# Block-sparse attention with a gated convolution feed-forward: mask rows copied in pieces, first loads in another turn, closing blocks in halves, and a new written order

## The chip, the core and the metric

The kernel is written for one core of a Trainium2 chip. A core has five engines that run side by side, each through its own list of instructions and strictly in that list's order: TensorE (PE: matrix products, with PEld for the loading of their weights), VectorE (DVE), ScalarE (ACT), GpSimd (POOL) and SyncE (SP). Here SP and POOL mainly start transfers between the memory and the core. Between engines only semaphores hold an instruction back. The metric is device time in microseconds (us) from the first to the last instruction of one launch, and what lies around it; the median over runs is compared.

## The reference

Attention over 4 batches, 8 heads, 768 positions and 64 numbers a head, with a mask of 32 by 32 blocks. Its output, heads side by side (512 numbers a position), goes through a feed-forward with a convolution over three neighbouring positions in its gate:

```python
scores = scale * np.matmul(q, k.transpose(0, 1, 3, 2))
...
mask = np.abs(blk_i - blk_j) <= window
mask = mask | (blk_i == 0) | (blk_j == 0) | (blk_i == n_blocks - 1) | (blk_j == n_blocks - 1)
for qb in range(n_blocks):
    for kb in sampled_blocks[qb]:
        mask[qb * block:(qb + 1) * block, kb * block:(kb + 1) * block] = True
...
attn = attn / (np.sum(attn, axis=-1, keepdims=True) + 1e-09)
return np.matmul(attn, v)
...
h = np.maximum(x @ w_in, 0.0)
...
for k in range(K):
    conv_out += conv_w[k][None, None, :] * hp[:, k:k + S, :]
gate = 1.0 / (1.0 + np.exp(-conv_out))
return (h * gate @ w_out)
```

The inputs and the output are in float32. The three sampled blocks of each row of blocks are drawn at random and are read by the kernel.

## The kernel before

Two heads make a pair; there are 16 pairs, four to a batch. For each pair a slot tensor `T_t` (five of them, 88 partitions by 24 by 128 in bf16) holds the transposed q in its first 12 chunks and the transposed k in its last 12, each in partitions 0 to 63. Partitions 64 to 87 hold 24 mask rows: one-hot block numbers of the keys, and for the queries a large negative number wherever a block is masked, so that one product over 88 rows gives masked scores. The mask rows depend on no head. They are built once in slot 0 and then copied to the other slots: `m_slot` (line 350) is one DVE copy of all 24 chunks for each of slots 1 to 4.

The queries of a batch are taken in two halves of 384 positions (g = 0 and 1; a chunk of q with an even number belongs to g = 0). In the first four pairs q and k come through POOL's transfers (`ld_k`, `ld_q`, `ld_v`, and `ld_q` again for g = 1), are transposed by PE (`k_tr`, `q_tr`) into a PSUM bank (`mix`, two of them) and copied from there into the slot (`k_cp`, `q_cp`, on DVE or ACT). The first pair is special: its q and k come in float32 through SP's and ACT's own transfers, are cast (`cast_q`, `cast_k`) and transposed head by head. Pairs 4 and 5 go the same way as 1 to 3; later pairs are transposed by a transfer and copied by `stg_cp`.

The work is cut into 144 units. A unit is some four `s` products into a bank `st` of two (`L754`), one exponential `exp` of 128x1024 on ACT from there (`L766`), and eight products `av` with the values (`L791`) into a bank `av` of two. The first 18 units are batch 0, g = 0, and 4.5 units belong to a pair: pair 1 begins in unit 4, pair 2 with unit 9 and pair 3 in unit 13. When the `av` of a pair are done, `rcp` and `norm` (`L700`, `L702`, DVE) divide by the sum and free the `av` bank; for the first segment `x_tr` and `x_cp` transpose the result on PE. After the four pairs of a segment come the feed-forward's first products `f1` (`L888`, bank `mix`), `relu` (DVE or ACT), the gate (`mul`, `add`, `tanh`, `g1`, `g2`), and the second products `f2` (`L823`), whose result `ev` copies to `o2s_t` and `out` sends to memory, 128 positions at a time.

Of the last batch the last block of 128 positions (t = 5) is made in two halves of 256 columns; blocks t = 3 and 4 are made whole. In the profile a group of `f2` in a whole block is 128x512, in a half 128x256.

No scheduler runs at build time. The order of all operations on all engines is written out in the string `ORDER`, two characters for an operation, then the engine where there is a choice (P, A, V, G) and the numbers of the buffers it takes. `put_down` (line 93) emits them in this order; within an engine the instructions stand as they do in the string. The lists of POOL and SP are part of it. At the start PE runs 42 products on zeros (`warm`, `fill`).

Of the kernel before, what the change touches and what calls it, by code (L numbers as in the profile page):

```python
# [25 lines left out]
6h1Z15U06u36z46C16D6i16q6r6E56L06v6M6w6A6B6j26k1+V1j5VV1n1/V6F6Q16R6G6l06N06S16O06V06P6W6H06I6mV6J16KV6X26T6+16U6/
ih070373074iiik1754181pijV00il7c1imV7d7e52b07h0in17iio6Y7j01s4V2U24W1t7m17n7o12cViF02dViGipV1iIiH4X2W24Y2X4Z1u4+1v
4/31050iq0ir7r06Z717s72767A1isA7t2iJiN17B7C32w12xV4781iO2yV771iz0iA7F07GiBA27H47f7g7k2p07K12z17L7l7p7q7P07Q7u7v2qV
2rViP79iK7M5it0iu7D07U12AV7w22BV2HV4ivV3iQ7V7R03337W17E7I7J7a17bV1iR810822K0832861iS2LV02MV7x877Niw17O7S7T883ixiL
iyV8b08c7X7Z07Y1847y0858g18d48hiM0iT7zV7+2N1898a8p08qiC08eiV22OV2PV2VV0iWiU8i58r08u18viD8f8z08A8w1102Y12Z02+3615134  # L30
373528B28j8k8s07/18E18F8t8x8y8J0iEV80V8l1j138miYj2iX8G38Kj908C8L48R18S8D8T58H8W08X8Ija8n18Y0j4iZ8/1908oV2/Vi+30Vj3
i/8M8N18U8V8Z94095jf1j5j08O291111962jg8+929c1939d9h09i97jbjh98j69e43c3d1523a1532C03f3e543l9m19nj732V1j83bV29901iji
jjV038V9j39o539V8P9ajc9r0jdA19sjo19w1jpjl09t0jqA9xjm9y1jnV3o9E09F9G23p03m22Q13rju19f09gjv9J19K2D09k9l9O09PjwA9L4jJ0
jLjK2EVjM9Q3jr19p9q2FVjNjO9T1jsjtVjR1jA09U9/0jB9ujS9V5jCA9vjx1jyjzAa09z9A1a41a59H9I9M2R09NjPjUjT9B1jZ29Cj/a10a619R
a90aa9S8Q29W9X2SVjV2TVjG1a20ae1jQj+ab2afjHa3jD0aj0a7aka8jWag4jEar1asal39Y2jIVk0jFVjXk539Zk1k6jYk8k7ackj1aw0axadahai
at0ay1amaB1aCan1aukv0avazaG0aHaD4k2aI3k9kak3k43q3h0jk9DaO1kk9baP3t13iaAkbao1kcaEaFkwaJaT0aKaL0aMaUkl3x3y03A3B2aQ5kx
aY1aV29+3u3s4ap3g3aq03jV3kVkykzA2kmaZb103D3C3Jb2knA3kB0kCkE1kFkDV14kGVkZ0k+a+0b313vVb61b7b84kN0kObe0aR1bfkQ1kRaSaW
aXk/kPA5bj1bkkK0bg3kSAbl5l0l1l2kLbo0kW1a/bpb0b4b5bt1b9buba0bq03M3N33K1aNbhld1kMVbv2kXbB0bCbikH0kYAbD13wVlf3nA3bG1kI
bb2lelg3zV4bckT1bmbnbr3P3OkJV6bH3UbI43F03Q13Gl52l7kUkVV7l3bL0bMl6bN3kp0kqbsbwbxbQ1bRbS5bV0bWbdkokrkd1bE1bX03R3E0ll3
lml8lol9lhlal41by1kAlblcbzlnlilpljc11ksbFbJbKbOc2c60c7c82ktA0bPbTbAkulk3HV3IVkekfkgc31cb0bUbYlt0lubZ0cccg1khA3lqlr  # L40
3LV0b+0lscd4lvlz1chlAco0cplBlCci3lwct1cuc4cq0lDA2lxA0cy0czc5lF13V03X3Y1403Zb/3+lGcv53SV13WV13TVlHVlI0lJcD1c9cElKV
m10m2m3cacem4m5cA1cF2lO1cfcI0cJcK4kilPlL0lMcjcklNAlQVm92ma410mbmcm6m7cl2cr1cQ1cRcS3cscwcV0cWcxcBcCcGcHlR0494a0c01ly
4f1c+1c/cX53/46472cLcN1mdd00lSd30d4lU1lVdb1dccOcmcncP42jelTAmelWVmh1mimjmfmkmgm84ed51dd2cM1cTcUcYcZlX0d1lYmllZVdg0
dhdi4l+1l/dl1d2dmd6d7dq0drm0Amp3de0d80dfdn34b4c4nds5mD1djdkdodpdv1dwdD0dEmx0mEmymmdx0mqd9msdtmrdudydz1dF2dI1dJmtmu
mnmo4o24s4ddGdHdN0dOdK4mvmzmFdadP34kdS1dTdLmwmGdMd+0d/dQmA4pdA24l143V2mHV344VmBV0dU5e31dRe4e00dVdWdX1dBe52e80e9mV1
mWea1mXV08dYmY0mZe10e2m+Vnh2ninknjed1ee4glEn21e6m/0ei0ejn0n34B4C34qef4ek3n4A4Geq1ere7ebecegehelev04r4y4Des0n1V9np0
nqnsnrewnl48V2en04hV3n51em1n6eteA1euex2n7Aa4t045dC2dZeBeon80mJ1eF0mKeGeC14z0n9mLnmeH4mMepeN1eOeS0eTmNA1naV4iV4mV34E
4F4MeP5ne0nb1nfeX1eyezeYeDeEeInx1nyntnzeU3nuf00eJncf1eZ04N24H1ngVnneK2eQ0eRmP0eVeWe+f514j4ueLeMf6f22ndAbe/f3fd0fe
f71mQmRnvno0nAnwnBnF3nGnInHfi1fjff4nCmC4vV4nD4wVnJf4mSmTA2nT1nUfn0fofk5f8f91fgo60o7fhfs1ftfp3fA0fBnK4Io8VnEmIfu0nL
fa1nMo30o4fC2flnVfmnWo5Vot2ouovowoxfb4AV4nXA0fF1fGfK0fLnN0nZ1nOfH1fM4oyfqfrnPn+n/AnQfP1fQo01fvo1nRA34JV04KVfwfU0fV  # L50
oz4OV0oAfR5oc0g01g1o2AfW3fx0fyol0omfD0fEfIfJodonoog20opoeAg50g6g72o91oaga1fNfOfSgbfTfXfY1gf0ggobVoB1oDoC4Loqgc1fZ2
oi0ojof1ognS4xnYgh4orosoEf+g3g4gn1g8gogs0ohAokAoFoJ3oKg9gp5gtmUfc0fzoR1gu3oX0gdoLgegigx1gyoMoNoGgjoSoHgG0gq0grgvgw
gHoYgz0gAgBgL1gMoOgI2gk1oIglgC0gN1oToZgQ0gRgS4f/gmoPoQo+gJ1o/A3mOgZ1oUg+h20h3g/5h43p70p8p9paoVV0pbV2h71h8gKpg1phpd0
p0pehg0gDgOpfV1cpiAhhh90pj1pm0pnhi2poAgPpkplAdhl1hmgThq0pp0gE1pqgUpB2pDpCpcpEpJ0pFhn1gFA1h00h1h5h6haps1pthbprAepGpK
pLpuAhrpMpv0hz1hApwhs4p11pHgV2gWhc1pNpxAfhB5hE0hdpR1pSpTpUp2gX0gYApOhj1hkp3p4hFpI1pVp5A1hG3hohphthuhN1py0he1pzhv0pP
hwhOhC0pQhfApAAhx1hDhHhW0hI1hyVqk0qlhP0hXpZ3hJ2p+p/pWqmAgqq1hQh/1qrhRq50hY2i0i80i9q6q0q1pXhKq2qsAhpYhS1q3q4hL1q7hZ0
q8i11ia4hMV2qh1qihTq9A3qB2qR0qCqDh+i2i31ibqn0qjAii40i5qt1qui61icid2qoi7Aqb1qcqpAjqwqviehU0qdhVVif0qeigAri0rjqJ3qEqx
qLqSqFqfA2r91raqyrkArbAqzqUrf0rgqGrc1rl0rmrhArA1rBp6qgoWqaqAqHqIrn1qKrorC2rdr30rv0rwrDrpreArq1rrrEqTqMrx1rs2qZ1rtqN
qOruryqVrzqPqQq+r4rR0rSrL1rMrNrOrTrUqWqXqYrPV1r5r6rVAr7A2q/r0rWrQr8r1V0r2rF0rGrHrIrJA3rK
# [52 lines left out]
def kernel(  # L112
# [207 lines left out]
    def dcopy(e, dst, src):  # L320
        if e == "ACT":
            nc.scalar.copy(out=dst, in_=src)  # L322
        elif e == "POOL":
            nc.gpsimd.tensor_copy(out=dst, in_=src)
        else:
            nc.vector.tensor_copy(out=dst, in_=src)  # L326
# [723 lines left out]
```

## Time and profile before

| what | value |
|---|---|
| time, median of 3 runs | 208.17 us (208.16 to 208.91) |
| the profiled execution's own time | 208.6 us |
| its span, first to last instruction | 206.6 us |
| mean granted clock of TensorE | 0.998 |
| busy: PE, DVE, ACT, POOL | 197.9, 187.0, 189.9, 61.1 us |
| instructions | 6225 |

The profile is a record of one execution. Its page gives busy times by engine, the span in 40 slices with the busy share in tenths, the transfers, and the chain of work that ended last. Further views show instructions in order of time (start, length, engine, line, operation, tiles; equal neighbours merged, in brackets the idle time before and what ended it), groups of instructions of one line and shape, and busy times in chosen stretches. Starts count from the first instruction.

### The profile page before, as it was taken

How to read it: one execution, taken by the hardware profiler on the slowest of the kernel's cores; microseconds unless marked ns; L12 is line 12 of the kernel's file. 1: busy time of each engine (PE TensorE's matmuls, PEld its weight loads, DVE VectorE, ACT ScalarE, POOL GpSimd, SP SyncE). 2: the span in 40 equal slices, each digit the busy share in tenths (PEclk: the TensorE clock that was granted, in tenths of full speed). 3: DMA queues.
4: the chain of work that ended last, by engine and by line, in shares of the span. 5: the costliest groups of instructions: out<-in, count | busy, mean ns of one | idle time of the engine just before them, and what ended most of it. 6: DMA issues, size and time to landing. Idle time of an engine off the chain costs nothing.

```text
span 206.6 us, 6225 instructions
## 1 busy us (share of the span) xinstructions
PE 197.9 (96%) x2400; PEld 142.8 (69%) x2418; DVE 187.0 (91%) x578; ACT 189.9 (92%) x250; POOL 61.1 (30%) x114
## 2 busy tenths in 40 slices
PE   7799999999999999999999999999999999999991
PEld 5577877787667766766576767676677767786750
DVE  7999999999999998999789989999999938999970
ACT  6999999999999999999979998999999979997841
POOL 8976655204353223217044153800000000000000
PEclk9999999999999999999999999999999999999999
DMA  6999999972949795999977659999133131010414
GB/s 160 179 196 188 187 172 132 156 127 41 113 59 184 109 194 87 145 151 173 194 98 98 142 76 181 138 137 162 47 111 91 22 121 51 3 51 5 152 54 152
DMA packets 49305, 25.00 MB, mean 121 GB/s; under 512 B 35100, under 2 KB 46332, under 8 KB 49276
## 3 DMA queue, kind: packets, MB, share of 16 engines
q0 software_dynamic: 20000, 11.24, 43.5%
q1 hardware_dynamic: 28988, 13.07, 30.2%
q8 instruction: 19, 0.31, 0.6%
q10 hardware_dynamic: 288, 0.30, 0.4%
q14 instruction: 10, 0.08, 0.2%
HBM read 23.09 MB, written 6.29 MB: 142 GB/s over the span
## 4 chain that ended last, share of the span: by engine, by line
PE 86%; DVE 5%; ACT 5%; issue 1%; another core or an unknown queue 1%; ACTq 0%
PE st L754 30%; PE mix L888 19%; PE mix L823 17%; PE av L791 17%; ACT pt L766 2%; DVE m L946 1%; DVE t L326 1%; PE mix L721 1%; ACT t L322 1%; PE st L823 1%; PE mix L517 1%; PE av L965 1%; ACT o2s L322 1%; DVE m L954 0%
## 5 line engine op out<-in xcount | busy, mean ns | idle before, releaser
L766 ACT ACTIVATE pt<-st 128x1024 bf16<-128x1024 f32 x144 | 140.3, 1036 | 2.6 <-PE st L754 1.8
L754 PE MATMUL st<-t 88*128 88x256 bf16 (+2 forms) x600 | 90.9, 268 | 1.8 <-ACT pt L766 0.7
L754 PEld LDWEIGHTS <-t 88*128 88x128 bf16 x600 | 48.2, 97 | 20.3 <-issue 2.2
L791 PEld LDWEIGHTS <-pt 128*128 128x128 bf16 x1152 | 52.8, 97 | 12.4 <-ACT pt L766 0.4
L791 PE MATMUL av<-vt,pt 128*128 128x65 bf16 x1152 | 58.9, 193 | 0.2
L888 PE MATMUL mix<-xT,winb 128*128 128x384 bf16 (+2 forms) x288 | 54.8, 308 | 0.3 <-ACT hE L908 0.2
L946 DVE TENSOR_SCALAR m<-hE,cw 128x382 bf16<-128x382 bf16 (+2 forms) x192 | 49.5, 317 | 0.4
L823 PE MATMUL mix<-woutb,gT 128*128 128x512 bf16 x166 | 45.3, 379 | 0.4
L954 DVE TENSOR_TENSOR m<-m 128x764 bf16<-128x764 bf16 (+2 forms) x64 | 33.8, 534 | 0.5
L888 PEld LDWEIGHTS <-winb 128*128 128x128 bf16 x288 | 24.1, 97 | 9.2 <-issue 0.8
L993 ACT ACTIVATE m<-m 128x764 bf16<-128x764 bf16 (+2 forms) x32 | 26.4, 830 | 1.3 <-DVE m L954 1.2
L823 PEld LDWEIGHTS <-gT 128*128 128x128 bf16 x200 | 17.4, 97 | 11.5 <-DVE gT L1001 0.6
L402 POOL COPY pace<-pt 1x1 bf16<-1x1 bf16 x24 | 8.4, 352 | 56.3 <-ACT pt L766 56.3
L910 DVE TENSOR_SCALAR hE<-mix 128x384 bf16<-128x384 f32 x29 | 16.0, 554 | 4.1 <-PE mix L888 3.2
L908 ACT ACTIVATE hE<-mix 128x384 bf16<-128x384 f32 (+2 forms) x35 | 17.1, 504 | 1.7 <-PE mix L888 1.7
L1001 DVE TENSOR_TENSOR gT<-m,hE 128x764 bf16<-128x764 bf16 (+3 forms) x36 | 18.2, 510 | 0.5
L702 DVE TENSOR_TENSOR xtok<-av,rcp 128x384 bf16<-128x384 f32 (+2 forms) x36 | 18.0, 507 | 0.4
L237 POOL DMA_DIRECT2D nat<-in_q_dram x23 | 17.2, 748 | 2.8 <-issue 2.1
L326 DVE COPY t<-mix 64x384 bf16<-64x384 bf16 (+1 forms) x34 | 13.9, 409 | 0.5
L322 ACT COPY o2s<-mix 128x512 f32<-128x512 f32 x17 | 9.9, 594 | 2.8 <-remote 2.0
L237 POOL DMA_DIRECT2D vn<-in_v_dram x16 | 11.6, 725 | 2.4 <-DVE vt L326 2.4
L996 DVE TENSOR_SCALAR m<-m 128x764 bf16<-128x764 bf16 (+3 forms) x36 | 11.9, 330 | 0.2
(73 smaller groups left out, 119.4 us busy)
## 6 DMA issues: line engine op xcount, KB each, us to landing
out_dram<-o2s SPq DMA_DIRECT2D x23, 256.0 KB, 3.1
vn<-in_v_dram POOLq DMA_DIRECT2D x16, 192.0 KB, 4.8
nat<-in_k_dram POOLq DMA_DIRECT2D x15, 192.0 KB, 4.2
nat<-in_q_dram POOLq DMA_DIRECT2D x6, 192.0 KB, 4.2
winb<-in_moe_w_in_dram POOLq DMA_DIRECT2D x2, 512.0 KB, 7.2
woutb<-in_moe_w_out_dram POOLq DMA_DIRECT2D x4, 256.0 KB, 5.8
nat<-in_q_dram POOLq DMA_DIRECT2D x9, 96.0 KB, 4.3
nq<-in_q_dram POOLq DMA_DIRECT2D x6, 96.0 KB, 5.2
```

Of the source, the lines that this page charges most:

```text
L237: return op(name, {eng: occ}, lambda e: on(e).dma_start(out=dst(), in_=src), prio, deps, dma=(kind, service), **kw)
L702: nm = op("norm", {"DVE": t_dps(128 * C)}, lambda e: nc.vector.tensor_tensor(out=xtok_t[xk.index][:, 0:C].rearrange("p c h d -> p h c d"), ...
L754: nc.tensor.matmul(out=st[:, 128 * x:128 * (x + n_)], lhsT=t[0:88, 12 + 6 * hh + kc, :], rhs=t[0:88, idx:idx + (n_ - 1) * (2 if P < NPE el ...
L766: nc.scalar.activation(out=pt_t[ptb.index][:, c0:c1], in_=st_t[stb.index][:, c0:c1], func=AF.Exp, bias=0.0, scale=0.125)
L791: nc.tensor.matmul(out=o[:, off:off + 65], lhsT=pt_t[ptb.index][:, 128 * x:128 * x + 128], rhs=V_t[vslot_b[P].index][:, hh, kc, 0:65], sta ...
L823: nc.tensor.matmul(out=acc(), lhsT=gT_t[gb.index][:, ffc, 128 * t:128 * t + 128], rhs=woutb[:, ffc, c0:c1], start=(ffc == 0), stop=(ffc == ...
L888: nc.tensor.matmul(out=mix_t[hb.index][:, w1 * y:w1 * y + w1], lhsT=winb[:, fc, 128 * ffc:128 * ffc + 128], rhs=xT_t[xt_buf[n].index][:, f ...
L908: nc.scalar.activation(out=dst, in_=src, func=AF.Relu, bias=0.0, scale=0.5)
L946: nc.vector.tensor_scalar(out=m_t[cb.index][:, x, y, 0:w], in0=hE_t[heb.index][:, f0 + y, t0 + x:t0 + x + w], scalar1=cw[:, x, f0 + y:f0 + ...
L954: nc.vector.tensor_tensor(out=m[:, a_, :, 0:w], in0=m[:, a_, :, 0:w], in1=m[:, b_, :, 0:w], op=ALU.add)
L993: th = [op("tanh", {"ACT": t_act(2 * w) + 0.04}, lambda e, cb=cb, w=w: nc.scalar.activation(out=m_t[cb.index][:, 0, :, 0:w], in_=m_t[cb.in ...
L1001: nc.vector.tensor_tensor(out=gT_t[gtb.index][:, f0:f0 + 2, t0:t1], in0=m_t[cb.index][:, 0, :, 0:w], in1=hE_t[heb.index][:, f0:f0 + 2, 1 + ...
```

## The change

- Slots 1, 2 and 3 get their mask rows by three smaller DVE copies each instead of one: `m_sk` (the 12 chunks of the keys), `m_sq` (the 6 chunks of the queries of g = 0) and `m_sr` (the 6 of g = 1). Products of g = 0 wait for the first two alone, products of g = 1 for the third too. Slot 4 gets its rows by a transfer of SP, `m_sp`.
- In POOL's list the turn of `ld_k`, `ld_q` of the first pairs and that of `ld_v` are no longer one chain, and the new order has the third pair's k and q (pair 2) ahead of the second pair's values (pair 1).
- Blocks t = 3 and 4 of the last batch are made in halves of 256 columns as t = 5 is: 27 `out` transfers where there were 25, 16 products of 256 columns for each 8 of 512.
- `ORDER` is another one throughout. In the first microseconds two copies of k of the first pair are on ACT and the first copy of q is on DVE, where it was the other way round; the two writings of g = 1 query mask rows into slot 0 (`m_q1`, `m_r1`) go from ACT, ahead of the first exponential, to DVE, behind the second pair's `norm`; the second part of the sampled mask (`a5`, second half) moves there too; the four `s` groups of the first two units stand together ahead of the second head's `q_tr`. By engine, DVE has 3 `ev`, 1 `q_cp`, `m_q1` and `m_r1` more and 2 `k_cp` and 1 `relu` fewer; 9 small mask copies stand for 4 whole ones.

```diff
+    def rows_to(s, c0, c1, step):
+        return lambda e: dcopy(e, T_t[s][64:88, c0:c1:step], T_t[0][64:88, c0:c1:step])
+
...
+    mask_g1 = {0: m_r}
     for s in range(1, NSLOT):
-        mr = [op("m_slot", {"DVE": 0.95}, lambda e, s=s: dcopy(e, T_t[s][64:88], T_t[0][64:88]),
-                 T(4.5 * s - 2.5), m_h1 + m_r, earliest=7.0 + 2 * s)]
+        mask_g1[s] = []
+        if s < NSLOT - 1:
+            mr = [op("m_sk", {"DVE": 0.53}, rows_to(s, 12, 24, 1), T(4.5 * s - 2.5), m_k + m_h1[1:]),
+                  op("m_sq", {"DVE": 0.33}, rows_to(s, 0, 11, 2), T(4.5 * s - 2.5), m_q + m_h1[:1])]
+            mask_g1[s] = [op("m_sr", {"DVE": 0.33}, rows_to(s, 1, 12, 2), T(12 + s), m_r)]
+        else:
+            mr = [dma("m_sp", "SP", lambda s=s: T_t[s][64:88].rearrange("j c s -> j (c s)"),
+                      T_t[0][64:88].rearrange("j c s -> j (c s)"), T(4.5 * s - 2.5), m_h1 + m_r, service=0.3)]
         mask_ready[(s, 0)] = mask_ready[(s, 1)] = mr
...
                 qk_ready[(P, hh, g)] = (two + qk_ready[(P, hh, "k")] + mask_ready[(min(s, NSLOT - 1), hh)] +
-                                        (m_r if P == 0 else []))
+                                        (mask_g1[min(s, NSLOT - 1)] if g else []))
...
-            in_turn("first" if P < NF else "v", lv)
+            in_turn("firstv" if P < NF else "v", lv)
...
-    ld_win[0].after.append(last_ld["first"])
+    ld_win[0].after += [last_ld["first"], last_ld["firstv"]]
...
-        halves = ((0, 256), (256, 512)) if last else ((0, 512),)
+        halves = ((0, 256), (256, 512)) if last or (b == B - 1 and t > 2) else ((0, 512),)
...
-                due + 3, [evo], uses=[ob], dma=("hw", 0.65 if not last else 0.4)))
+                due + 3, [evo], uses=[ob], dma=("hw", 0.65 if len(halves) == 1 else 0.4)))
```

More of the change, by code (lines that the diff above doesn't have):

```diff
@@ L26 @@
[L26 to L59, printed above, removed]
+0J1f0O0K1k00021030405060708090a0b0c0d0e0f0g0h0i0j010P1W01X0Q1U00R2810S0+A1CA2290/V2610T13V1g1h1i1j0I1EA1G00k0l0m0n
@@ new lines @@
+jf0jg971jaj935V36Vjbj5j69a09b8/jm9394989i1999j9c29d9n09ojn9ejhjc9k49p59s19t9u13a3d3b2583g1592I03i3j23l3k5a3r3s23u
+3v02W238V18U2jdje118V9f0joji9x09y9l0jjA0jpV19g3eV3fV1o3hV29z3jr1jsju0jv9C1jtAjwAjP0jQjRjS9D9E0jx19m9K09L9qjA09P19Q
+jy9r9M29R4jzVjT9U09V9v9W59w2J19A9BjB2KV2LV9FjCAjU9H19IjX19G19N9O9Z19+jG1a50jD0a6jEjH9/1a73jVjYjZjFVjWj+aa1jIAab9S
+2X0af09T9X9YagjM12YV2ZVj/k32ac0ak1aljNjJ0jKa0a1ah4am53x3w3D3G3m38W23n03o9Jk0jOVk4a22k5k1k6jLVk2k7kb3a3kckdkeap0aq
+ax1a80a9adaeayaikp1ar2aC0az1aDkB0aE3ajkCaH1aIanaM0aoaNk8aJ0kfk9aO4kgasat1aAkqaBaFaU1aGaVaKaZ0aLa+aPaQaW5a/23z13y49h
@@ new lines @@
+4J4K4Lew1eheiemn80enexn9ey5ereB0eCne1es1eG1nfnaV4oVnpeHeD0ngAet2nv2nwnxnreunyeI24S4T0ezeAnb0eL0eMnceEeFeJeT1eUnk1
+eN3ndAanleY0nh0nieZeKeOePeV4nmAnD1nFnEnzeQ0nGeR4Ae3eveS4N1ko4OmInsnjAbe+1mP1f11f2mQf35mRmV0f60f7eW0nAnL3nHntnMnOnN
+nPf80mSmWeXfb1fcmXmYe/f0nB4BV4mTV3fd3nInu0nJ4sV34CVf4f5f9fj0fkmZA2fl2fo1fao91feoafpoc0odff1fq4fmft0fnnQobVnKoeVoz0
+nCnRoAoCfufv1o31fy1o60o4fzo7frfG0o5AnZ1fHn+n/fA5o8AfI04GV4nSor1osotfg1fhoB4PV0ou4QVfL1fMfsfwfxo0fQ0fN3o1A0fRfBof0
+fV1fS2oi1fCfWojf+0ogfJ0f/fKfOokVovoDfD2fX4ohAg61g7ol1omg01g85oH2oIonVowfEoo0opfPfTgb0fUoqVgcgd0oEgg1nT1nUghgi3nVfY
@@ L60 @@
+qIqX0qYhZq+qZi51i6qb1qcie0ifqdhR0i73hSA2i30ig2i4qeqn0qoi8qfA0i91qpAiia2ibihiiqt1ic0quqKqz2ij0qBqAikidAqh0qvAjqih+1
+qjh/Vil1qkimAru1rvqCqP3qQqDqJq/qLqlA3rl0rmrwAqErnAqFrr1rsrtAqMro0rx0ryqGqRqSqNrz2rArprqAqOqmqgpcm+rBr31rH1rIrC0rD
+r90rE1rJ2qTqUr0rFrKrGqVrLqWr1r4rarM0s70s11s8s2rNs3rO1r2rPr5s9r6rQr7A3rbs4sarcs5V0sbArdA1rf1rgrhrirR0rjVr8s6rerSrTrU
+rX1rVA2rkscrWrYrZr+r/As0
 """
@@ L421, in kq_transposes @@
             cq = [cast("cast_q", lambda x=x: nat_t[nb.index][:, 0, 192 * x:192 * x + 192],
-                       lambda x=x: qf[:, 192 * x:192 * x + 192], -16.5 + 2 * x, [ld_q0[x]], {"ACT": 0.25, "DVE": 0.28},
+                       lambda x=x: qf[:, 192 * x:192 * x + 192], -16.5 + 2 * x, [ld_q0[x]],
+                       {"ACT": 0.25, "DVE": 0.28, "POOL": 0.45} if x else {"ACT": 0.25, "DVE": 0.28},
                        alloc=[] if x else [nb], uses=[nb] if x else []) for x in range(2)]
```

30 lines of the change are left out of this document (25 added, 5 removed).

## The prediction

> **What bounds the kernel now.** I read the page first: busy shares, then the 40 slices, then the chain of waits.
>
> ```profile
> span 206.6 us, 6225 instructions
> PE 197.9 (96%) x2400; PEld 142.8 (69%) x2418; DVE 187.0 (91%) x578; ACT 189.9 (92%) x250; POOL 61.1 (30%) x114
> ...
> DVE  7999999999999998999789989999999938999970
> ...
> PE 86%; DVE 5%; ACT 5%; issue 1%; another core or an unknown queue 1%; ACTq 0%
> ```
>
> PE is busy for 96% and makes 86% of the chain, and the change takes no product away. So only three things can move: when PE's dense stretch begins, what it loses inside, and what follows its last product. But DVE and ACT are above 90% too, and DVE's slices stand at nine from the first microseconds. Busy times by stretch say where each engine has room:
>
> ```profile
> 7.00:27.00 20.00, 19.29 (x296) 15.27 (x294) 18.93 (x60) 19.85 (x23) 14.17 (x27) 1.00 1.31 188
> 27.00:47.00 20.00, 19.66 (x280) 15.39 (x278) 19.47 (x57) 19.41 (x23) 6.85 (x13) 1.00 1.08 141
> 87.00:107.00 20.00, 19.89 (x215) 13.20 (x216) 17.84 (x50) 19.12 (x25) 6.88 (x12) 1.00 0.90 155
> ```
>
> The columns are stretch, length, then PE, PEld, DVE, ACT, POOL, granted clock, transfers. Up to 47 us DVE has about 0.5 to 1.1 us of idle time in 20, no more than the gaps between its instructions. In the early stages a DVE instruction that is added is paid; around 100 us there are 2 us in 20 to hide it.
>
> **The head, as ACT sees it.** The view in order of time, ACT alone:
>
> ```profile
> 5.54 0.60 ACT L322 COPY t<-mtok 24x128 bf16<-24x128 bf16 x2 [0.69 <-DVE mtok L294]
> 6.17 0.47 ACT L322 COPY t<-mix 64x384 bf16<-64x384 bf16 x1
> 6.66 0.51 ACT L322 COPY t<-mtok 24x384 bf16<-24x384 bf16 x1
> 7.20 0.35 ACT L322 CAST nat<-o2s 128x192 bf16<-128x192 f32 x1
> 7.57 0.51 ACT L322 COPY t<-t 24x384 bf16<-24x384 bf16 x1
> 8.10 1.02 ACT L766 ACTIVATE pt<-st 128x1024 bf16<-128x1024 f32 x1
> ```
>
> The first exponential starts at 8.10 behind `m_q1` (6.66) and `m_r1` (7.57). The change takes both off ACT, 1.02 us. In exchange ACT gets two k copies, 0.47 each by the row at 6.17, and loses the q copy of that row. The first k copy falls into ACT's idle 0.69 ahead of 5.54, the other stands where the q copy stood. DVE reaches the mask half about 0.16 later, because three memsets stand in front of it. So ACT's two mask copies end at 6.14 + 0.16 = 6.30, the k copy at 6.79, the cast at 7.16, and the first exponential starts at about 7.2, **0.9 us earlier**. Its products have their q copy (0.35 on DVE, behind the mask half that let ACT go at 5.54) at 5.5 + 0.16 + 0.35 = 6.0, and are done by 7.0.
>
> **What DVE makes of that.** An early exponential is worth something only if the next pairs are ready early. These rows of DVE and PE show that they just were:
>
> ```profile
> 8.37 1.22 DVE L326 COPY t<-t 24x3072 bf16<-24x3072 bf16 x1
> ...
> 12.20 0.95 DVE L326 COPY t<-t 24x3072 bf16<-24x3072 bf16 x1
> 13.18 0.36 DVE L326 COPY vt<-vn 128x768 bf16<-128x768 bf16 x1
> ...
> 14.04 1.87 DVE L326 COPY t<-mix 64x768 bf16<-64x768 bf16 x4
> ```
> ```profile
> 15.98 0.61 PE L754 MATMUL st<-t 88*128 88x384 bf16 x4
> 16.41 0.98 DVE L326 COPY t<-t 24x3072 bf16<-24x3072 bf16 x1
> ...
> 23.46 0.56 DVE L702 TENSOR_TENSOR xtok<-av,rcp 128x384 bf16<-128x384 f32 x1
> ...
> 26.20 0.38 PE L754 MATMUL st<-t 88*128 88x256 bf16 x2
> ```
>
> Pair 2's copies end at 15.91 (14.04 and 1.87) and unit 9's products start at 15.98: there DVE set the pace. Prices of the copies, from the groups by shape:
>
> ```profile
> L326 DVE COPY t<-mix 64x384 bf16<-64x384 bf16 x24 | 8.4, 350 | 0.3
> L326 DVE COPY t<-t 24x3072 bf16<-24x3072 bf16 x4 | 4.1, 1024 | 0.1
> L326 DVE COPY t<-t 24x768 bf16<-24x768 bf16 x1 | 0.4, 351 | 0.0
> L326 DVE COPY t<-t 24x384 bf16<-24x384 bf16 x1 | 0.3, 284 | 0.0
> L326 DVE COPY t<-nblk 24x384 bf16<-24x384 bf16 x1 | 0.5, 487 | 0.0
> L294 DVE SCALAR_TENSOR_TENSOR mtok<-sbi,keyid,A 24x384 bf16<-24x384 int32 x2 | 1.1, 606 | 0.0
> ```
>
> Between 768 and 3072 elements the price grows by 0.29 ns each, so `m_sk` (24x1536) is 0.575. `m_sq` and `m_sr` (24x768, every second chunk) lie between 0.351 (the same size in one piece) and 0.57 (two strided copies of 24x384); I take 0.40, nearer the lower end, since 0.284 plus 384 more elements gives that. A slot then costs 0.575 + 2 x 0.40 = 1.375 in place of 1.02: over three slots 4.13 for 4.10, slot 4's copy being gone. In total nothing; in time the copies stand earlier.
>
> Up to pair 2's copies the new list has lost the second mask half (0.61), two k copies (0.70), two whole slot copies (1.22 + 0.95) and pair 1's value copy (0.36): 3.84. It has gained a q copy (0.35), three `m_sk` (1.73) and three `m_sq` (1.20): 3.28. Pair 2 is ready 0.5 earlier, at 15.4, and the lead of 0.9 is down to about 0.5.
>
> Up to the third pair's `norm` (23.46 to 24.02) it has lost the k copies (0.70) and three slot copies (1.22 + 0.95 + 0.98): 3.85. It has gained the q copy and six mask copies (3.28), four q copies of g = 1 (1.40), `m_q1` (0.49, the `nblk` row), `m_r1` (0.28), one `m_sr` (0.40) and an `x_cp` (0.35): 6.20. So this `norm` ends 2.35 later, at 26.4. In PE's list its transposes stand directly ahead of the products that began at 26.20, and everything of PE waits behind them: `s`, `av`, and so the next exponentials. By the sum those products start near 26.6, 0.4 late; with the copies at their lower ends (0.48 and 0.35, and the rows above overlap a little) it is 25.9, and with the transposes 26.15, no change. I take the lower end, **0.0**: the lead of the start is used up by DVE at unit 20. Bounds for the head: -0.9 (nothing of it lost) to +0.6 (upper ends).
>
> The Trainium skill (VectorE: DVE Perf Modes, "The TRN2 errata — SBUF-src ops pay a fixed extra latency per instruction") says that a vector instruction from on-chip memory pays a fixed part each time, so that small pieces pay it once per piece. Its formula, 58 cycles and a quarter of the elements at 0.96 GHz, would give an estimated 0.46 and 0.26, six early copies 2.16 and not 2.93; the `norm` would end near 25.6 and 0.4 of the lead would survive, 207.2 in all. The row of 24x768 has 0.351 for the 0.26, so I keep to the rows.
>
> **Loads and SP.** Pair 1's values go from the fourth to the sixth place on POOL, and their copy on DVE to behind pair 2's.
>
> ```profile
> 5.90 0.75 POOL L237 DMA_DIRECT2D vn<-in_v_dram x1
> vn<-in_v_dram POOLq DMA_DIRECT2D x16, 192.0 KB, 4.8
> SPq L237 <- PE st L754: 21.4, 2, 21.0
> ```
>
> Landed 4.8 after an issue no later than 5.90, they are there by 10.7, and the fourth unit's `av` comes after 12. Nothing. If they were late, PE would wait in that `av`. The new `m_sp` waits on SP for `m_r1` (about 23); behind it stand the query rows of later slots and the transposing transfers. SP before stood 21.0 us in one wait for the first slot to come free, so this lies in it. Nothing; without that cover, the time of one transfer ahead of pair 6.
>
> **The tail.** The last block before is one copy of 512 columns, then its transfer:
>
> ```profile
> 202.71 0.58 ACT L322 COPY o2s<-mix 128x512 f32<-128x512 f32 x1 [1.97 <-remote]
> L322 ACT COPY o2s<-mix 128x512 f32<-128x512 f32 x17 | 9.9, 594 | 2.8 <-remote 2.0 <-PE mix L823 0.7
> L322 ACT COPY o2s<-st 128x256 f32<-128x256 f32 x1 | 0.4, 372 | 0.7 <-PE st L823 0.7
> 204.40:204.80 0.40, 0.00 (x0) 0.00 (x0) 0.00 (x0) 0.00 (x0) 0.00 (x0) 1.00 1.02 384
> L823 PE MATMUL st<-woutb,gT 128*128 128x256 bf16 x16 | 1.9, 273 | 0.0
> ```
>
> In halves the last copy is 0.372 for 0.594: 0.22 less. The last transfer's 256 KB (128x512 f32) move at 384 GB/s in the stretch shown; half of them take 0.34 us less. The half before it is finished eight products earlier (16 halves take 1.9 us in the last row, so 0.9), and SP is free again. PE pays nothing: two products of 256 columns at 1.9/16 = 0.12 stand for one of 512. The tail gives **-0.55**. Bounds: -0.8 (the copy starts earlier as well) and +0.2 (the gate ends last in the new order and PE waits for it).
>
> **In between.** DVE takes three block copies more, at most 3 x 0.69, `m_q1`, `m_r1` and a q copy, and loses two k copies and a `relu`: about +1 us in all. It lies in the room that the stretch at 100 us shows; without it, it is 1 us. The other stalls that PE shows belong to one order:
>
> ```profile
> 36.62 0.33 PE L517 MATMUL mix<-ident,nat 128*128 128x128 bf16 x3 [0.34 <-DVE t L326]
> 109.57 0.60 PE L754 MATMUL st<-t 88*128 88x128 bf16 x4 [0.47 <-ACT pt L766]
> 193.30 0.83 PE L888 MATMUL mix<-xT,winb 128*128 128x128 bf16 x12 [0.20 <-ACT hE L908]
> ```
>
> A new order loses these and has others. Near 34 us I see one: a `q_tr` that needs the bank of the third `relu`, which stands late on DVE. I put the balance at 0, bounds -1.0 (all three gone) and +1.0 (as many again).
>
> **Sum.** 0.0 - 0.55 + 0 = -0.55. The profiled execution took 208.6 with a span of 206.6; the median of the runs shown is 208.17, 0.4 below it, and the difference carries over. Forecast: 208.17 - 0.55 = **207.6**.
>
> **Rivals.**
> - *The head's lead survives.* The mask copies cost their lower ends, the `norm` is in time, 0.5 of the lead (unit 9's) reaches the dense stretch, and half of the 1.0 of stalls goes. For it: ACT's rows, whose 1.02 is certain. Against it: DVE's full slices. 208.17 - 0.55 - 0.5 - 0.5 = 206.6.
> - *DVE becomes the bound up to about 60 us (the slower side).* One mechanism: DVE's list up to the second `relu` holds all nine mask copies (4.13), a q copy, two q copies of g = 1, `m_q1` and `m_r1` (1.82) for four slot copies and two k copies (4.80): 1.1 late where the feed-forward begins, and PE's `mix` banks wait. It decides as soon as DVE is later there than PE's spare room, which ends at 27 us by the stretches. If the ca. 1 us of added work falls there as well: 208.17 - 0.55 + 1.1 + 1.0 = 209.7.
> - *The halves don't bring what they should*: the last gates end later and PE waits 0.5 for them ahead of its last groups: 208.1.
>
> **Chances.** Forecast 0.40 (its own range 206.9 to 208.4), lead survives 0.26, DVE the bound 0.23, halves idle 0.11. 0.5% of 208.17 is 1.04 us, about what a measurement of this kernel tells from no change: faster is below 207.13, slower above 209.21. Faster: nearly all of the second case and a good third of the forecast, 0.39. Slower: most of the third case, 0.21. Same: 0.40. The range, from the unknown ends, 206.0 to 209.6.
>
> **What would show it.** Right: first exponential near 7.2; pair 2's products near 15.5; the transposes after the third `norm` waiting for DVE, and the products behind them at 26.0 to 26.6; the last copy 0.37 long and the end some 0.55 sooner after PE's last product. Wrong: products behind the third `norm` before 25.7 (then the lead survived), `m_sq` at 0.5 or above, idle time of PE ended by DVE summing to over 1 us between 28 and 60 us, or by `gT` in the last 8 us.

## The result, and the profile after

| | before | after |
|---|---|---|
| time, median of 4 runs each | 208.21 us (208.16 to 208.91) | 210.28 us (210.17 to 211.58) |
| ratio, with 95% interval | | 1.0104 (1.0065 to 1.0142) |
| span of the profiled execution | 206.6 us | 209.8 us |
| its mean granted clock | 0.998 | 0.992 |

The change makes the kernel 2.1 us slower (1.4 to 3.0 by the interval); 207.6 was forecast, and 210.28 lies above the range as well. The profiled execution of after is its longest one, 211.58: in it TensorE's clock fell to half for 3.4 us (last section). Four more executions have spans of 208.4 to 208.6 at a clock of 1.0, so that drop hardly moves the median (210.22 without it). Where times behind 12 us matter I therefore read a second profile of the same kernel, "after again", with a span of 208.7 and a clock of 1.0.

The page of after, to lay beside that of before:

```profile
span 209.8 us, 6287 instructions
PE 201.9 (96%) x2434; PEld 145.7 (69%) x2434; DVE 188.8 (90%) x586; ACT 189.8 (90%) x249; POOL 60.2 (29%) x114
...
PEclk9969999999999999999999999999999999999999
...
PE 57%; DVE 35%; ACT 4%; issue 2%; ACTq 0%
...
L920 ACT ACTIVATE hE<-mix 128x384 bf16<-128x384 f32 (+2 forms) x36 | 17.9, 504 | 1.4 <-DVE gT L1013 1.1
```

The shares of busy time tell nothing: PE stands at 96% as before. Two other rows do. DVE makes 35% of the chain of waits where it made 5%. And the group of ScalarE's `relu` has idle time put down to the gate's product `gT` on DVE, 1.1 us. The second row is the one that led to the cause; DVE's share of the chain is no measure of the loss, as trials 7 and 13 below show. The `relu` row of before names another releaser, the products it reads:

```profile
L908 ACT ACTIVATE hE<-mix 128x384 bf16<-128x384 f32 (+2 forms) x35 | 17.1, 504 | 1.7 <-PE mix L888 1.7
```

**The head.** ACT of after in order of time, then DVE's mask copies:

```profile
5.70 0.60 ACT L323 COPY t<-mtok 24x128 bf16<-24x128 bf16 x2 [0.20 <-DVE mtok L295]
6.32 0.47 ACT L323 COPY t<-av 64x384 bf16<-64x384 bf16 x1
6.82 0.35 ACT L323 CAST nat<-o2s 128x192 bf16<-128x192 f32 x1
7.27 1.94 ACT L778 ACTIVATE pt<-st 128x1024 bf16<-128x1024 f32 x2
```
```profile
7.25 0.55 DVE L327 COPY t<-t 24x1536 bf16<-24x1536 bf16 x1
...
8.43 0.54 DVE L327 COPY t<-t 24x768 bf16<-24x768 bf16 x1
...
10.89 0.89 DVE L327 COPY t<-t 24x768 bf16<-24x768 bf16 x2
```
```profile
L327 DVE COPY t<-t x2: 425/482/539, 10.9 to 11.2; 24x768 bf16<-24x768 bf16 x1, 24x1536 bf16<-24x1536 bf16 x1
```
```profile
8.17 0.35 DVE L327 COPY t<-t 24x768 bf16<-24x768 bf16 x1
```

The first exponential starts at 7.27 where it started at 8.10. `m_sk` costs 0.55, and the first `m_sq` 0.54. The row at 10.89 merges two neighbours of different size: the second fence, the same two copies by shape, has an `m_sq` of 0.43 and an `m_sk` of 0.54. The third fence is the first `m_sq` in after again, 0.35. Over the eleven profiles with the new list the 24x768 pieces take 0.35 to 0.70, and each profile has some at 0.35; what makes single ones longer stays open. What becomes of the early start shows on PE in after again:

```profile
11.95 0.40 PE L803 MATMUL av<-vt,pt 128*128 128x65 bf16 x8 [0.42 <-DVE vt L327]
...
15.50 0.61 PE L766 MATMUL st<-t 88*128 88x384 bf16 x4 [0.21 <-DVE t L327]
...
26.66 0.34 PE L733 MATMUL mix<-ident,xtok 128*128 128x128 bf16 x3 [0.68 <-DVE xtok L714]
26.84 0.38 PE L766 MATMUL st<-t 88*128 88x256 bf16 x2
```

Pair 2's products start at 15.50, and the transposes behind the third `norm` wait 0.68 us for DVE. The lead is gone: the products behind them start at 26.84, in before at 26.20. On the way PE's first `av` also waits 0.42 us, for DVE's copy of its values.

**The loss.** Late in the kernel stands the wait that the page's `relu` row counts. After again, around 187 us, on ACT, DVE and PE:

```profile
186.40 0.87 ACT L1005 ACTIVATE m<-m 128x764 bf16<-128x764 bf16 x1
188.38 0.60 ACT L920 ACTIVATE hE<-mix 128x512 bf16<-128x512 f32 x1 [1.10 <-DVE gT L1013]
188.87 1.01 ACT L778 ACTIVATE pt<-st 128x1024 bf16<-128x1024 f32 x1
```
```profile
186.76 0.55 DVE L1013 TENSOR_TENSOR gT<-m,hE 128x764 bf16<-128x764 bf16 x1
187.31 0.36 DVE L1008 TENSOR_SCALAR m<-m 128x764 bf16<-128x764 bf16 x1
...
187.70 0.56 DVE L1013 TENSOR_TENSOR gT<-m,hE 128x764 bf16<-128x764 bf16 x1
```
```profile
187.86 0.60 PE L835 MATMUL mix<-woutb,gT 128*128 128x512 bf16 x2
189.03 0.22 PE L733 MATMUL mix<-ident,xtok 128*128 128x128 bf16 x1 [0.57 <-ACT hE L920]
```

Read backwards: PE's transpose at 189.03 takes the `mix` bank that the `relu` reads. The `relu` starts at 188.38, when the second `gT` product (187.70 and 0.56) is through, though ACT is free from 187.27. That product reads `hE_t` (line 1015 of after's code) and this `relu` writes it (line 909). By the code they touch the same two of that tensor's eight blocks, but different columns in them: the `relu` belongs to the next segment and writes columns 385 to 640, the product reads 1 to 382. So neither needs anything of the other; the trace names the product as what the `relu` waits for all the same. In the new `ORDER` the `relu` stands behind the product, in the old one ahead of it. Behind the `relu` stands an exponential, so ACT's list moves as a whole.

**The tail.** The last two copies in after's view of ACT:

```profile
205.74 0.37 ACT L323 COPY o2s<-mix 128x256 f32<-128x256 f32 x1 [1.32 <-PE mix L835]
206.62 0.37 ACT L323 COPY o2s<-mix 128x256 f32<-128x256 f32 x1 [0.50 <-PE mix L835]
```

From the start of the last copy to the end of the span it is 209.8 - 206.62 = 3.2 us, where it was 206.6 - 202.71 = 3.9.

### The profile page after: what moved, and what is told of

It reads as the page before. It is cut to its first block, busy times and chain, and to the rows that moved or that the text cites. A ratio compares the mean times of both kernels' runs of the same rounds, so it can differ in the third digit from the quotient of the medians.

```text
span 209.8 us, 6287 instructions
## 1 busy us (share of the span) xinstructions
PE 201.9 (96%) x2434; PEld 145.7 (69%) x2434; DVE 188.8 (90%) x586; ACT 189.8 (90%) x249; POOL 60.2 (29%) x114
## 4 chain that ended last, share of the span: by engine, by line
PE 57%; DVE 35%; ACT 4%; issue 2%; ACTq 0%
PE st L766 16%; PE mix L835 15%; PE mix L900 12%; PE av L803 9%; DVE t L327 8%; DVE m L958 7%; DVE m L966 4%; DVE xtok L714 3%; DVE hE L922 3%; PE av L229 2%; DVE gT L1013 2%; ACT pt L778 2%; DVE diag L385 2%; DVE m L1008 2%; DVE xT L327 1%
## 5 line engine op out<-in xcount | busy, mean ns | idle before, releaser
L766 PE MATMUL st<-t 88*128 88x256 bf16 (+2 forms) x600 | 94.1, 269 | 0.5 <-ACT pt L778 0.3
L803 PEld LDWEIGHTS <-pt 128*128 128x128 bf16 x1152 | 55.6, 97 | 14.8 <-issue 1.9
L803 PE MATMUL av<-vt,pt 128*128 128x65 bf16 x1152 | 62.5, 193 | 0.6 <-DVE vt L327 0.5
L900 PE MATMUL mix<-xT,winb 128*128 128x384 bf16 (+2 forms) x288 | 55.6, 307 | 0.9 <-DVE o2s L327 0.4
L958 DVE TENSOR_SCALAR m<-hE,cw 128x382 bf16<-128x382 bf16 (+2 forms) x192 | 51.1, 324 | 1.0 <-ACT hE L920 0.9
L835 PE MATMUL mix<-woutb,gT 128*128 128x512 bf16 (+1 forms) x200 | 49.0, 362 | 0.3 <-DVE hE L922 0.2
L835 PEld LDWEIGHTS <-gT 128*128 128x128 bf16 x216 | 18.5, 97 | 10.9 <-issue 0.8
L413 POOL COPY pace<-pt 1x1 bf16<-1x1 bf16 x24 | 7.1, 297 | 55.1 <-ACT pt L778 55.0
L920 ACT ACTIVATE hE<-mix 128x384 bf16<-128x384 f32 (+2 forms) x36 | 17.9, 504 | 1.4 <-DVE gT L1013 1.1
L922 DVE TENSOR_SCALAR hE<-mix 128x384 bf16<-128x384 f32 x28 | 15.5, 552 | 2.9 <-PE mix L900 2.9
L323 ACT COPY o2s<-mix 128x512 f32<-128x512 f32 (+1 forms) x16 | 8.8, 549 | 4.2 <-PE mix L835 4.2
```

The costliest lines, as they stand in the source:

```text
L766: nc.tensor.matmul(out=st[:, 128 * x:128 * (x + n_)], lhsT=t[0:88, 12 + 6 * hh + kc, :], rhs=t[0:88, idx:idx + (n_ - 1) * (2 if P < NPE el ...
L803: nc.tensor.matmul(out=o[:, off:off + 65], lhsT=pt_t[ptb.index][:, 128 * x:128 * x + 128], rhs=V_t[vslot_b[P].index][:, hh, kc, 0:65], sta ...
L835: nc.tensor.matmul(out=acc(), lhsT=gT_t[gb.index][:, ffc, 128 * t:128 * t + 128], rhs=woutb[:, ffc, c0:c1], start=(ffc == 0), stop=(ffc == ...
L900: nc.tensor.matmul(out=mix_t[hb.index][:, w1 * y:w1 * y + w1], lhsT=winb[:, fc, 128 * ffc:128 * ffc + 128], rhs=xT_t[xt_buf[n].index][:, f ...
L958: nc.vector.tensor_scalar(out=m_t[cb.index][:, x, y, 0:w], in0=hE_t[heb.index][:, f0 + y, t0 + x:t0 + x + w], scalar1=cw[:, x, f0 + y:f0 + ...
```

## The experiments

Each was timed beside runs of before on the same chip, and the ratio is to those. Edits of the order are shown as operations, one line each, where the string itself would tell nothing. `s#53` is the 54th `s` operation in the numbering of the code, the last of unit 26. By the count of `s` products in after again it starts at about 33 us, `s#193` at about 120 us (the expectations say 135) and `s#281` at about 183 us. Mixtures keep the computation.

**1. The same kernel again** (`after_again`).

> The changed kernel once more. In its first profile the granted clock was 0.5 from 12.3 to 15.7 us and the span was 209.8, while the unprofiled runs agree on 210.2. Theory 'clock': the dip belongs to the new head and comes back, span 209.5 to 210. Theory 'DVE and order': the dip was chance and no part of the median; clock 1.00, span 208.5, the first exponential at 7.3, pair 2's products at about 16, and PE again idle for 0.4 to 0.6 ahead of the transposes of the third norm near 26.5.

Measured: 210.48 at a clock of 1.0, span 208.7. The drop of the clock in the first profile did not come again, and the loss is there without it.

**2. Only the halves, in the old order** (`b_halves`).

```diff
-halves = ((0, 256), (256, 512)) if last else ((0, 512),)
+halves = ((0, 256), (256, 512)) if last or (b == B - 1 and t > 2) else ((0, 512),)
 f2 of t = 3 among t = 5
+now only its first half; the second half behind t = 5
 f2 of t = 4, in halves
```

> The kernel before, its own order, with blocks t = 3 and 4 of the last batch in halves and nothing else. Prediction's term: -0.55, so 207.6 (ratio 0.9974). If the halves bring what the changed kernel's profile shows behind its last product (3.2 in place of 4.1 us): -0.9, 207.3 (0.9957). Rival (PE or SP pays for the halves): 208.2 or more.

Measured: 208.53, ratio 1.0001 (0.9986 to 1.0015). Nothing was gained. The trace says in part why. In it the last copy starts 3.3 us ahead of the end (203.02 of 206.3), so the saving is there; but the weight loads of the products wait for the gate twice, in before (second fence) once:

```profile
197.02 1.67 PEld L823 LDWEIGHTS <-gT 128*128 128x128 bf16 x16 [0.28 <-DVE gT L1001]
199.03 0.55 PEld L823 LDWEIGHTS <-gT 128*128 128x128 bf16 x5 [0.34 <-DVE gT L1001]
```
```profile
199.46 0.55 PEld L823 LDWEIGHTS <-gT 128*128 128x128 bf16 x4 [0.33 <-DVE gT L1001]
```

My order had moved the second half of t = 3 to the end. Before, those products lay between the gate products and covered the first of the two waits. The trial mixed two things, and number 8 takes them apart.

**3. The new head with the old rest, and 4. the old head with the new rest** (`a_head_b_rest`, `b_head_a_rest`).

```diff
 a_head_b_rest: operations of after up to s#53
-operations of after behind it
+operations of before behind it, closing blocks whole
 b_head_a_rest: operations of before up to s#53
-operations of before behind it
+operations of after behind it, closing blocks in halves
```

> New mask copies, new loads and the new order up to unit 26 (its second group of products), then the old order and old closing blocks. Theory 'head' (DVE's list of small copies and late norms costs the 2 us): 209.5 to 210.3 plus the halves' share, at least 209.8. Theory 'rest' (the new order behind unit 26 costs them): 207.9 to 208.6.

> Old mask copies, old loads and the old order up to unit 26, then the new order with the closing blocks in halves. Theory 'head': 207.3 to 207.8, the gain of the halves left alone. Theory 'rest': 209.5 to 210.3.

Measured: the new head 208.46, ratio 0.9991 (0.9971 to 1.0012); the new rest 210.50, 1.0087 (1.0066 to 1.0107). The nine small copies, the loads in another turn and SP's transfer cost nothing, and gain nothing that can be told. The new head is everything up to about 33 us. The whole loss lies behind unit 26.

**5. and 6. The seam moved to `s#193` and to `s#281`** (`a193_b_rest`, `a281_b_rest`), both from after's order into before's, closing blocks whole.

> The changed order up to the 194th pair of score products (about 135 us), then the order of before to the end, closing blocks whole. Theory (the loss behind unit 26 is a sum of separate waits, read off the gaps between TensorE's products: +0.39 us from 30 to 65, +0.18 from 65 to 110, +0.30 from 110 to 135, +0.63 from 135 to 160, +1.16 from 160 to 190, +0.29 behind that, and -0.85 behind the last product): 0.9 us above the kernel with only the new head, so 209.3. Rival (the loss is all in the last 75 us, where slack is least): 208.5. Rival (the new order loses evenly and the cover that it uses up early comes due at the end whichever order stands there): 210 or more.

> The changed order up to the 282nd score product (about 183 us), then the order of before, closing blocks whole. Theory of separate waits: the wait of 0.74 us at 189 us and what follows it are gone, the earlier ones (0.39 + 0.18 + 0.93) stay, and so does the long closing: 208.5 + 1.5 = 210.0. Rival (the loss lies before 183 us and the end only shows it): 210.5 or more, because the closing in halves is gone too.

Measured: 209.61, ratio 1.0044 (1.0023 to 1.0065), and 210.82, 1.0090 (1.0058 to 1.0122). The first comes 0.3 above the theory, and its trace has a wait that neither parent has: a PE stall ended by DVE at 126.55, 0.71 us, some 6 us behind the seam. Without that stall some 0.4 of its 1.1 us above the new head are left for the new order between 33 and 120 us, an estimate within the intervals' width. The second is not decided: its median falls to the rival, its interval, 210.1 to 211.4 on the 208.87 beside it, reaches down almost to the theory's 210.0, and of its four executions one had the drop of the clock.

**7. One instruction earlier** (`a_relu`).

```diff
 exp 141 (ACT), tanh 27 (ACT)
+relu 59 (ACT)
 g1 27 (DVE), rcp 33 (DVE), g2 27 (DVE, the gT product)
-relu 59 (ACT)
```

> The changed kernel with one instruction put down earlier: the ScalarE relu of slot 24's fourth group (relu#59) ahead of the add and the gT product of group 27, where the old order has it, so that it need not wait for that product. Theory: that one relu holds the exponential and the bank of the next transpose, and TensorE's wait of 0.74 us at 189 us is its price; it goes and so does part of the 0.34 behind it: 209.4 to 209.7. Rival (the wait only moves to the next late instruction of VectorE): 210.2 to 210.4.

Measured: 209.74, ratio 1.0039 (1.0020 to 1.0058), span of the profiled execution 207.2. ACT and PE there:

```profile
185.94 0.87 ACT L1004 ACTIVATE m<-m 128x764 bf16<-128x764 bf16 x1
186.67 0.64 ACT L919 ACTIVATE hE<-mix 128x512 bf16<-128x512 f32 x1
187.15 1.06 ACT L777 ACTIVATE pt<-st 128x1024 bf16<-128x1024 f32 x1
```
```profile
187.39 0.60 PE L834 MATMUL mix<-woutb,gT 128*128 128x512 bf16 x2
187.83 0.22 PE L732 MATMUL mix<-ident,xtok 128*128 128x128 bf16 x1
```

The `relu` follows `tanh` with nothing between, and the transpose follows the products. The wait is gone, and the list of PE's waits between 184 and 203 us is empty. The product `gT` now starts at 187.34, right behind the `relu`'s end (187.31), so the pair is ordered either way round. DVE's share of the chain is still 34%.

**8. Only the very last block in halves** (`b_t4_halves`).

```diff
-halves = ((0, 256), (256, 512)) if last else ((0, 512),)
+halves = ((0, 256), (256, 512)) if last or (b == B - 1 and t == 4) else ((0, 512),)
```

> The kernel before with its very last closing block alone in halves, all else in its old order. The first trial of halves moved the second half of the block before it to the end as well, and TensorE then stood 0.5 us more between 195 and 201 us. Theory (halves do save what lies behind the last product, 4.15 us to 3.32, and that order paid it back on TensorE): 0.8 us less than before, 207.4 to 207.6. Rival (the saving is eaten by the extra copy and transfer wherever they stand): 208.2 to 208.4.

Measured: 208.29 against 208.87, ratio 0.9966 (0.9952 to 0.9981), so 0.4 to 1.0 us. The median lies in the rival's range, but both ranges had been reckoned from a lower time of before; against the before beside it the saving is near the theory's 0.8. Its last copy:

```profile
202.95 0.37 ACT L322 COPY o2s<-mix 128x256 f32<-128x256 f32 x1 [2.05 <-PE mix L823]
```

206.3 - 202.95 = 3.35 us to the end, for 3.9 before. The halves are worth what lies behind the last product, as long as they leave the products ahead of them in place.

**9. to 12. Late part alone, with repairs, and after without halves** (`b193_a_rest`, `b193_a_relu_ev`, `a_relu_ev`, `a_whole`).

```diff
 b193_a_rest: new head, order of before up to s#193, then that of after
 b193_a_relu_ev: the same, and
+relu 59 ahead of g1 27, as in 7
+ev 10 (DVE, copies an output block) ahead of
 stg_cp 16 (DVE)
-ev 10
 a_relu_ev: after with the same two lines
 a_whole: after, t = 3 and 4 whole
```

> The new head to unit 26, the order of before up to the 194th score product (about 135 us), then the changed order to the end, closing blocks in halves. Theory of separate waits: only those behind 135 us are left (0.63 with the wait for the copy of an output block near 143 us, 1.16 with the relu at 189 us, 0.29 in the closing, -0.85 behind the last product): 208.46 + 1.2 = 209.7. Rival (the early loss matters and the late one follows from it): 208.5 or less. Rival (all of the loss comes behind 135 us): 210.3.

> The same mixture with two instructions put down earlier: the relu as in the kernel with only the relu moved, and the VectorE copy of output block 10 ahead of the cast of a staged block (stg_cp#16) that now stands before it. Theory of separate waits: 0.74 and some 0.7 behind it go at 189 us as they did there, 0.36 at 143 us goes, the gain behind the last product stays: 209.7 - 1.4 - 0.36 = 207.9 to 208.3, no slower than before. Rival (VectorE is the bound there, and the cast comes late in place of the copy): 208.6 to 209.2.

> The changed kernel with both instructions put down earlier. Theory: 0.3 to 0.4 us less than with the relu alone (209.74): 209.3 to 209.5, span 207.5 to 207.9 at full clock. Rival (the cast is late instead): 209.7 or more.

> The changed kernel with its closing blocks whole, as in before (the same order otherwise). If the halves save in the new order what they saved alone at the end of the old one (0.85 us behind the last product less what TensorE stands longer): 210.35 + 0.6 = 210.9 to 211.2. Rival (they only move the wait in front of the last product, as in the first trial of halves): 210.2 to 210.5.

| | median, us | ratio | interval |
|---|---|---|---|
| b193_a_rest | 210.21 | 1.0080 | 1.0056 to 1.0104 |
| b193_a_relu_ev | 208.73 | 1.0007 | 0.9988 to 1.0027 |
| a_relu_ev | 209.42 | 1.0042 | 1.0018 to 1.0065 |
| a_whole | 210.94 | 1.0107 | 1.0084 to 1.0131 |

The part behind `s#193` alone brings back nearly the whole loss, 0.0080 of the 0.0087 to 0.0104: the theory's 209.7 was 0.5 too low, and the last rival, 210.3, came near. Two instructions out of some 6,300 take it away again, 0.0073 of 208.7, or 1.5 us. The second of the two does nothing by itself: after with both stands at 1.0042 where after with the `relu` alone stood at 1.0039 (its median falls into the theory's range only because the before beside it was 0.14 lower). The views show that its wait moved on. The first fence is PE of after again, the second PE of `a_relu_ev`, after with both repairs:

```profile
143.61 0.48 PE L900 MATMUL mix<-xT,winb 128*128 128x384 bf16 x2 [0.36 <-DVE o2s L327]
```
```profile
147.01 0.81 PE L899 MATMUL mix<-xT,winb 128*128 128x384 bf16 x4 [0.35 <-DVE hE L921]
```

So for this copy the rivals were right, and the mixture stayed at 208.73 where the theory had 208.3 at most: DVE is nearly full there. Busy times by stretch, after again and then the kernel with the new head and the old rest (stretch, length, PE, PEld, DVE):

```profile
135.00:150.00 15.00, 14.64 (x147) 9.34 (x146) 14.84 (x44) 14.25 (x20) 0.20 (x1) 1.00 0.92 116
150.00:185.00 35.00, 35.00 (x420) 25.22 (x418) 30.27 (x96) 32.69 (x45) 0.00 (x0) 1.00 0.20 60
185.00:192.00 7.00, 6.25 (x82) 4.68 (x80) 6.13 (x24) 5.86 (x10) 0.00 (x0) 1.00 0.01 2
```
```profile
135.00:150.00 15.00, 15.00 (x174) 10.15 (x172) 14.62 (x44) 14.99 (x20) 0.00 (x0) 1.00 0.76 110
150.00:185.00 35.00, 35.00 (x425) 25.64 (x424) 30.17 (x96) 33.59 (x50) 0.00 (x0) 1.00 0.22 66
185.00:192.00 7.00, 7.00 (x79) 4.86 (x78) 6.83 (x32) 5.25 (x10) 0.00 (x0) 1.00 0.01 4
```

At 135 to 150 us DVE is busy for 14.84 of 15, and there one copy put earlier came with a wait for another instruction. A full DVE alone costs nothing, though: with the old rest it is busy for 14.62 of 15 and for 6.83 of 7, and PE never stands. In after it is busy for 6.13 of 7 around 189 us, and there the place of one instruction was all. And without its halves after is at 210.94, as the theory had it, but 1.0107 against 1.0085 to 1.0104 for the orders with halves doesn't tell what they are worth. The views do for the end: from the start of the last copy it is 209.4 - 205.59 = 3.8 us to the end without halves, 208.7 - 205.52 = 3.2 in after again, 0.6 less.

**13. One instruction later, in the kernel before** (`b_relu_late`).

```diff
 tanh 27 (ACT)
-relu 59 (ACT)
 g2 26, rcp 33, g1 27, g2 27 (DVE)
+relu 59 (ACT)
 x_tr 12 (PE)
```

> The kernel before with one instruction put down later: the ScalarE relu of the fourth group of the last slot but one put behind the gT product of VectorE that the changed order has ahead of it, ahead of the transpose that takes its bank. Theory (place alone sets the price): the relu can start at about 186.5 instead of 185.4 us, the transpose that stands right behind its end now (186.09) comes 1.0 us later, TensorE waits 0.7 to 1.1 us there, and no later slack takes it back: 209.3 to 209.8. Rival (only in the new order, where VectorE is late anyway, does it cost anything): 208.5 to 208.9.

Measured: 210.09, ratio 1.0052 (1.0036 to 1.0069), 0.8 to 1.4 us. ACT and PE in it, then PE of before:

```profile
187.04 0.60 ACT L908 ACTIVATE hE<-mix 128x512 bf16<-128x512 f32 x1 [1.10 <-DVE gT L1001]
```
```profile
187.69 0.22 PE L721 MATMUL mix<-ident,xtok 128*128 128x128 bf16 x1 [1.02 <-ACT hE L908]
```
```profile
185.80 0.60 PE L823 MATMUL mix<-woutb,gT 128*128 128x512 bf16 x2
186.24 0.22 PE L721 MATMUL mix<-ident,xtok 128*128 128x128 bf16 x1
```

The price can be read in before's own trace, from its ACT and DVE:

```profile
185.53 0.62 ACT L908 ACTIVATE hE<-mix 128x512 bf16<-128x512 f32 x1
```
```profile
186.19 0.56 DVE L1001 TENSOR_TENSOR gT<-m,hE 128x764 bf16<-128x764 bf16 x1
```

From the `relu`'s start at 185.53 to the end of the product at 186.75 it is 1.2 us. The place sets the price by itself, in an order that has nothing else late. (The median is above the theory's 209.8, with a before of 208.85 beside it; the 1.1 us by the ratio lie within the 0.7 to 1.1 of waiting that it names.) DVE's share of the chain is 4% here and 5% in before. The same 1.10 us of ACT waiting for `gT` appears as in after, PE waits 1.02 for the bank, and no later slack takes it back.

**14. The new head and the last block in halves** (`a_head_b_t4`).

> The new head to unit 26, the order of before behind it, the last closing block alone in halves. If the two add up: 208.46 - 0.6 = 207.8 to 208.0, ratio to before 0.994 to 0.997. Rival (one of them uses what the other frees): 208.3 to 208.7. If the new head brings the drop of the clock, one or two of its executions have a mean granted clock of 0.992 or less and are over 1 us longer; if that was chance, none.

Measured: 207.92 against 208.85, ratio 0.9960 (0.9944 to 0.9976). It beats both kernels, as the eighth did; that the head adds to the halves can't be told from the two intervals. None of the six executions had the drop of the clock; at the rate of the last section, 9 in 78, that is about as likely as not, so it decides nothing.

## Why the prediction was wrong, step by step

- **The head, 0.0: right in the time, in part by luck.** First exponential near 7.2: 7.27. Pair 2's products near 15.5: 15.50. The transposes behind the third `norm` waiting for DVE and the products behind them at 26.0 to 26.6: 0.68 us of waiting, products at 26.84, so 0.64 late, beyond even the upper bound of 0.6. The 0.42 us that the first `av` waits has no term. Alone the head came out at 0.9991 all the same. One profile of each kernel shows where that may come from: behind 27 us PE's waits sum to 1.0 us in before and to 0.4 with the new head alone, though the order behind unit 26 is the same. No trial shows that this is the whole of it. Of the prices, `m_sk` (0.575) came to 0.55 in most profiles, `m_sq`, taken as 0.40 between 0.351 and 0.57, to 0.35 to 0.70, and the six early copies together to 3.04 and 3.06 in the two profiles of after, for 2.93. The formula quoted from the Trainium skill (VectorE: DVE Perf Modes, "The TRN2 errata — SBUF-src ops pay a fixed extra latency per instruction") made 2.16 of them, further off than the nearest row of the trace; the same section says that the formula comes out low for a single instruction.
- **The loads and SP, nothing: right,** with the head.
- **The tail, -0.55: right.** Behind the start of the last copy 3.9 us became 3.2. Alone in place it was 0.4 to 1.0 us by the times; in the new order only the views tell, 0.6.
- **In between, 0 with bounds of 1.0 either way: this step failed.** It says of the stalls "A new order loses these and has others", and prices the others by the number and size of those that before's trace shows, 0.20 to 0.47 us each. The runs put about 1.9 us behind `s#193` (1.0080 against 0.9991), and that is already net of the 0.6 us that the halves save. Even the three upper bounds together, 1.8 us, would have ended at 209.97. One single wait makes 1.0 to 1.5 of it, shown in three ways: it goes when the `relu` of after goes earlier (1.0087 to 1.0104 down to 1.0039), it goes in the late part alone (1.0080 to 1.0007, with the other repair), and it comes into before when the `relu` goes later (1.0052). It had no row in before, because there the same `relu` stands ahead of the product, with no wait. Stalls of the old trace bound nothing here. What did hold it was the two orders: an instruction that writes a tensor had been put behind one that reads it, if in other columns, with an exponential and a PSUM bank queued behind.
- **DVE's added work, "about +1 us in all": mis-summed.** By its own prices three block copies (2.07), `m_q1`, `m_r1` and the q copy (1.12), less two k copies (0.70) and a `relu` (0.55 by before's rows), make 1.9; DVE's busy time rose by 1.8, from 187.0 to 188.8. "It lies in the room that the stretch at 100 us shows" does not hold for 135 to 150 us, where DVE has 0.16 us of room in 15 and PE stood for `o2s` and, once that was mended, for `hE`. What these waits cost was not shown apart from the rest.
- **The rivals.** The slower one, DVE as the bound up to 60 us, came near the time (209.7) by another road. From 33 to 120 us the new order costs some 0.4 to 0.7 us (the seam trial less its own stall; 1.0042 against 1.0007); the intervals of these ratios overlap, so this is likely but not shown. That the lead survives was wrong: the products behind the third `norm` came 0.64 us late. That the halves don't bring what they should happened in trial 2, for the reason that this rival gives, but not in the change.
- **The signs.** "Idle time of PE ended by DVE summing to over 1 us between 28 and 60 us" did not come; nor did the predicted stall near 34 us, a `q_tr` for the bank of the third `relu`. "`m_sq` at 0.5 or above" came in the first profile of after (0.54) and not in the second. PE did not wait for `gT` in the last 8 us. No sign was named for anything between 60 us and the last 8 us, which is where the loss was.

What stays open: single causes for the rest of the late part (1.9 us and the 0.6 that the halves give, less the `relu`, leaves about 1 us), of which only the wait that wanders from 143 to 147 us has a name; and whether the wait of the `relu` would go if the segments lay in tensors of their own, since the columns of `hE_t` that it and the product touch are different ones already. That wasn't tried.

## What to carry to other kernels

When a written order is replaced, go through pairs of instructions on different engines that write and read one tensor, in different columns too, and look for those whose turn is now the other way round: in the trace of the old kernel such a wait has no row, and where a bank and an exponential queued behind it, it cost its full length here. Its price stands in the old trace as the distance from the start of the one to the end of the other, here 1.2 us, and ScalarE's wait was then 1.10. Halving the last transfer paid here as long as the products that covered the last gates stayed where they were.

## What the runs showed of the hardware

TensorE's granted clock fell to half for 3.4 us while there was work for it. Stretches of the first profile of after (columns as in the prediction: behind the length PE's busy time, and the granted clock third from the end):

```profile
9.00:12.00 3.00, 2.32 (x19) 1.44 (x19) 2.88 (x7) 2.76 (x4) 1.95 (x3) 1.00 1.40 191
...
12.50:15.50 3.00, 3.00 (x30) 2.37 (x28) 2.27 (x7) 1.79 (x2) 2.86 (x6) 0.50 1.42 201
...
15.75:16.00 0.25, 0.25 (x9) 0.25 (x7) 0.14 (x1) 0.11 (x1) 0.23 (x2) 1.00 1.49 192
```

PE had been busy for 2.32 of the 3 us before, with one wait of 0.49 us that ended at 12.22; the wait of 0.42 in after again, at the same `av`, brought no drop. The Trainium skill (TensorE: Matmul & The Clock Gate, "Part 1: The HAM clock gate") lets the clock fall after an idle window of about 3.4 us. The length of the drop, 12.3 to 15.7, fits that window; the idle window does not appear in the trace. Over all runs listed here, 9 of 78 executions with the new head had a mean clock of 0.992 or less, and none of 100 with the old head fell below 0.995; these nine are 0.7 to 1.7 us longer than the medians of their kernels. What in the new head brings it on was not found.
